# Batch 1's third and fourth pair of heads: k and v loaded through GpSimd's DMA queue instead of SyncE's

## The chip, the core and the metric

The kernel runs on one core of a Trainium2 chip. The core has a matrix engine (PE, or TensorE), a vector engine (DVE), a scalar engine (ACT), GpSimd (POOL) and SyncE (SP), each with its own stream of instructions that it works off in order. They meet through semaphores. DMAs are issued by instructions on SP, ACT or POOL; each issuer has its own queue. The metric is the time on the device in microseconds; a run here is compared by the median of several executions.

## What is computed

The reference is a linear attention with a norm, followed by a feed-forward layer:

```python
batch, n_heads, seq, head_dim = (8, 8, 576, 64)
kv  = np.einsum('bhsd,bhse->bhde', k, v)
out = np.einsum('bhsd,bhde->bhse', q, kv)
rms = np.sqrt(np.mean(out * out, axis=-1, keepdims=True) + 1e-06)
out = out / rms * g_norm
x = out.transpose(0, 2, 1, 3).reshape(4608, 512)
h = x @ w_in                      # 512 -> 2048
g = np.maximum(0.01 * h, h)
return g @ w_out                  # 2048 -> 512
```

The weights come as 64-bit floats and are rounded to 32 bits by the kernel itself.

## The kernel before

**Tiling.** The 4608 tokens are nine blocks of 512 rows. A batch has 576 tokens, so a block's x takes one batch's outputs and a piece of the next. The eight heads of a batch are four pairs: `load_pair(b, p)` loads k, v and q of pair p of batch b. A k or v load is 288 KB into a tile of the tags `k_in` and `v_in` (`in_tile`, two buffers of each); q goes in four pieces into `q_in`. Each of these loads is a DMA on SP's queue (L130 for k and v through `load_two`, L159 for q). Batch 0 is loaded apart, by `load_first`, over three queues.

**Attention of a batch.** `attention(b, ...)` is a generator; whoever builds the program takes one step of it at a time. It turns q (L455, DVE), multiplies k by v for two pairs at a time (`attention_kv`, 72 PE records that the profile names `kv_ps`), copies the sums to `kv` (`copy_kv`, L324, DVE), then makes outputs (PE `o_ps`; ACT squares L368 and scaled copies L374 for 448 columns, L416 and L421 for the 128 columns that fall to the next block), and divides by the norm (DVE L372 to L402, ACT L386 and L394). It also asks for the loads of later pairs: after the first two pairs of batch b it asks for pairs 2 and 3 of the same batch, after the last two for pairs 0 and 1 of the next. For batches from 2 on (`apart`) these go into a list, `to_load`, that is worked off one by one. Batch 1 is the only one with `apart=False`: it asks for its pairs 2 and 3 at once, in the step after the first kv group.

**The first block.** `first_block` works on block 0 in the plain way, in sixteen steps n = 0 to 15, since the weights are still coming in. Step n makes `h_ps` from x and one w1 tile (128 of the 2048 columns), ACT applies the leaky relu (L1055), and one step later four accumulators `o_acc` take the product with one w2 tile. Between the steps, `between(n, half)` runs: it takes a step of attention (batch 0's tail, then batch 1 at the places 12 to 28), issues weight loads on SP (L220) and rounds weights that have landed.

**The weights.** There are 32 tiles (16 of w1, 16 of w2). A raw tile is 512 KB, and there are seven homes for raw tiles, three in `stage`, four in `pairs`. `round_f64` turns a raw tile into the 32-bit tile: ACT reads it twice (L247, L245, into `add` and `cut`), DVE makes four steps of it (L249, L253, L255, L258). A w1 tile is a part of `w1_all`, called `w_all` in the profile; w2 tiles are called `w`. The last tiles in order are those of w1 for n = 14, w2 for 13, w1 for 15, w2 for 14, w2 for 15.

**The sums on POOL.** From block 1 on, the products are made in Strassen's way, with seven products for eight. The weight sides for it are sums of tiles (`add`, L636), which POOL makes in the homes that raw tiles leave: `sides_w1`, `sides_w2`, `combine`. The sums that are needed again go to DRAM from SP's queue (L685, L723 to L727).

**What sets the order.** The order of PE's matmuls, of the loads, and of the four rounding steps is pinned to the program. Where `in_turn` and `add` do not pin (they pin only once `steady` is true, from block 2 on, or for `in_line`), a scheduler places the instructions of DVE, ACT and POOL by its own estimate of when their inputs come. So the order on these engines between the pinned instructions is no part of the text of the kernel.

Of the kernel before, what the change touches and what calls it, by code (L numbers as in the profile page):

```python
# [23 lines left out]
def kernel(  # L24
# [36 lines left out]
    nc = tc.nc  # L61
# [31 lines left out]
    def in_turn(ins):  # L93

        if steady or in_line:
            pin(ins)
# [24 lines left out]
    k_ins, v_ins, q_ins = {}, {}, {}  # L121

    def half_of(p, i):


        return i ^ (p & 1)

    def load_two(eng, src, t):

        pin(eng.dma_start(t.rearrange("p j d -> p (j d)"),  # L130
                          src.rearrange("h (p j) d -> (h p) (j d)", j=J)))
        return t

    def in_tile(name):
        return ins.tile([P, J, D], F32, tag=f"{name}_in", name=f"{name}_in")
# [3 lines left out]
    def load_some(n=1):  # L139

        while to_load and n > 0:
            b, p, what = to_load.popleft()
            load_pair(b, p, what)
            n -= 1

    def load_pair(b, p, what="kvq"):


        if "k" in what:
            k_ins[b, p] = load_two(nc.sync, k[b, 2 * p:2 * p + 2], in_tile("k"))  # L150
            v_ins[b, p] = load_two(nc.sync, v[b, 2 * p:2 * p + 2], in_tile("v"))
        if "q" not in what:
            return
        t = ins.tile([P, T * D], F32, tag="q_in", name="q_in")
        for l in range(2):
            for c in range(2):
                r0, n = 64 * l + 32 * c, T * D - 32 * c
                src = q[b, 2 * p + half_of(p, l)].rearrange("(t s) d -> t (s d)", s=T)
                pin(nc.sync.dma_start(t[r0:r0 + 32, :n], src[:, 32 * c:]))  # L159
        q_ins[b, p] = t  # L160
# [151 lines left out]
    def attention_kv(b, m, kv_ps):  # L312

        two = [(k_ins.pop((b, p)), v_ins.pop((b, p)), p) for p in (2 * m, 2 * m + 1)]
        for j in range(J):
            for i in range(2):
                for k_in, v_in, p in two:
                    r, c = 64 * i, 64 * half_of(p, i)
                    matmul(kv_ps[p % 2][c:c + 64], lhsT=k_in[r:r + 64, j, :],
                           rhs=v_in[r:r + 64, j, :], start=(j == 0), stop=(j == J - 1))  # L320

    def copy_kv(b, kv_ps):
        for i in range(2):
            in_turn(nc.vector.tensor_copy(kvs[b % 2][:, i::2, :], kv_ps[i]))  # L324
# [14 lines left out]
    def kv_tiles():  # L339
        return [ps_att.tile([P, NP // 2, D], F32, tag="att", name="kv_ps") for _ in range(2)]  # L340
# [83 lines left out]
    def tail_of(b, lo, hi, fine=False, kv=(None, None)):  # L424
        sums = []
        if hi - lo <= N2:
            both_outputs(b, lo, hi, sums, kv[0])
            yield
            if kv[1] is not None:
                kv_beside(b + 1, kv[1], att_tiles("kv_ps"))  # L430
            yield
        else:
            for e in range(2):
                outputs(b, lo, hi, e, sums, kv[e])
                yield
        for _ in divide(lo, hi, sums):
            if fine:
                yield
        if not fine:
            yield  # L440
# [3 lines left out]
    def kinds(b):  # L444
        return ("q",) if b > KV_BESIDE else ("q", "kv")

    def attention(b, apart=True, fine=False):

        qT = qTs[b] = work.tile([P, NP, S], F32, tag="qT", name="qT")
        beside = b > KV_BESIDE  # L450
        kv_ps = None if beside else kv_tiles()

        def turn(p):
            q_in = q_ins.pop((b, p))
            in_turn(nc.vector.transpose(  # L455
                qT[:, p, :].rearrange("p (t s) -> p s t", s=T),
                q_in.rearrange("p (s d) -> p s d", d=D)[:, :, :32]))

        for m in range(2):
            turn(2 * m)  # L460
            yield
            turn(2 * m + 1)
            if m:
                yield
            if kv_ps:
                attention_kv(b, m, [t[:, m, :] for t in kv_ps])
            pairs_next = [(b + m, p) for p in ((2, 3) if m == 0 else (0, 1)) if b + m < B]
            if b == KV_BESIDE and m:
                to_load.extend((b + 1, p, "kv") for p in range(2))
            if apart or m == 0:  # L470
                for nxt in pairs_next[:1 if apart else 2]:
                    if apart:
                        to_load.extend((*nxt, what) for what in kinds(b + m))
                    else:
                        load_pair(*nxt)
            yield
            if apart:
                if m and kv_ps:
                    copy_kv(b, kv_ps)
                for nxt in pairs_next[1:]:  # L480
                    to_load.extend((*nxt, what) for what in kinds(b + m))
                yield
        if not apart:
            copy_kv(b, kv_ps)
            yield
        kv = [(None, None), (None, None)]
        if KV_BESIDE <= b < B - 1:
            kv = [(None, None), (0, 1)] if b > KV_BESIDE else [(None, 0), (None, 1)]
        tails = [tail_of(b, max(i * NT, b * S), min((i + 1) * NT, (b + 1) * S), fine, kv[i - b])
                 for i in (b, b + 1)]  # L490
        if not fine:
            for tail in tails:
                yield from tail
            return

        for tail in (0, 0, 0, 0, 0, 1, 0, 0, 1, 1, 1, 1, 1, 1):
            next(tails[tail])
            yield
# [538 lines left out]
    def first_block(between):  # L1037
# [28 lines left out]
        for t in range(4):  # L1066
# [3 lines left out]
            else:  # L1070
# [3 lines left out]
    first_attention()  # L1074
    steps = {i: tail for tail in [tail_of(0, NT, S)] for i in (6, 8, 10)}
    a_steps = attention(1, False)
    steps.update((i, a_steps)
                 for i in (12, 13, 15, 16, 18, 20, 22, 23, 24, 26, 28))
    loaded, rounded = 7, 5

    def between(n, half):
        nonlocal loaded, rounded
        go(steps.get(2 * n + half, iter(())), 1)

        while half and rounded < min(3 * n + 8, 2 * n + 13, len(w_jobs) - (n < 11)):
            if loaded < len(w_jobs):
                load_w(loaded)
                loaded += 1
                if loaded in (15, 19):
                    load_pair(1, (loaded - 15) // 4)  # L1090
            round_w(rounded)
            rounded += 1
        if (n, half) == (12, 0):
            for p in range(2):
                load_pair(2, p)
# [38 lines left out]
    for i in range(1, NB):  # L1134
        one = i == 1
        steady = not one
        late, a_steps = a_steps, attention(i + 1, fine=not one) if i + 1 < B else iter(())
        os = {}
        for c in range(NC):
# [113 lines left out]
```

## Time and profile before

| what | value |
|---|---|
| median of 8 runs | 917.81 us (915.93 to 922.62) |
| the profiled execution's own time | 918.2 us |
| its span | 916.5 us |
| granted TensorE clock | 1.0 of full |
| PE busy, 70 to 90 us | 18.07 of 20 us |
| PE busy, 90 to 142 us | 52.00 of 52 us |
| PE busy, 230 to 900 us | 669.86 of 670 us |
| DMA engines busy, 105 to 142 us | 49% |
| POOL busy, 70 to 90 us | 0.00 us |
| POOL busy, 105 to 142 us | 16.33 of 37 us |

The span runs from the first to the last instruction of the program; the profiled execution's time has 1.7 us more around it. Times within the span are counted from its start. A line of a timeline has the start and the length in us, the engine, the line of the kernel, the operation, what it writes and reads, and the number of instructions merged; what ended the idle time before it stands in brackets. The matmul lengths are modelled and overlap, so distances from start to start are the safer measure on PE.

The stretch of 27 to 142 us is first_block. Up to about 110 us the DMA engines are full: weights, and batches 1 and 2, come in one after another. From 142 us on PE has work without a gap up to the end.

### The profile page before, as it was taken

How to read it: one execution, taken by the hardware profiler on the slowest of the kernel's cores; microseconds unless marked ns; L12 is line 12 of the kernel's file. 1: busy time of each engine (PE TensorE's matmuls, PEld its weight loads, DVE VectorE, ACT ScalarE, POOL GpSimd, SP SyncE). 2: the span in 40 equal slices, each digit the busy share in tenths (PEclk: the TensorE clock that was granted, in tenths of full speed). 3: DMA queues.
4: the chain of work that ended last, by engine and by line, in shares of the span. 5: the costliest groups of instructions: out<-in, count | busy, mean ns of one | idle time of the engine just before them, and what ended most of it. 6: DMA issues, size and time to landing. Idle time of an engine off the chain costs nothing.

```text
span 916.5 us, 18030 instructions
## 1 busy us (share of the span) xinstructions
PE 908.6 (99%) x6976; PEld 775.7 (85%) x6976; DVE 633.0 (69%) x1168; ACT 328.4 (36%) x645; POOL 370.0 (40%) x438
## 2 busy tenths in 40 slices
PE   8999999999999999999999999999999999999998
PEld 5444447888998999899999999999999999999997
DVE  5876995587457876587756786678659755755565
ACT  5454433242135233433243323332443333223330
POOL 2000354977633473226421642264226422642222
PEclk9999999999999999999999999999999999999999
DMA  8999926895599778766886789658755676666632
GB/s 260 234 252 217 271 82 192 275 304 167 169 351 289 230 212 266 235 229 213 257 258 217 221 249 272 221 174 207 249 181 176 190 222 198 183 190 222 198 108 92
DMA packets 90229, 200.06 MB, mean 218 GB/s; under 512 B 9888, under 2 KB 42272, under 8 KB 90144
## 3 DMA queue, kind: packets, MB, share of 16 engines
q1 hardware_dynamic: 79680, 187.04, 69.1%
q10 hardware_dynamic: 10016, 10.69, 3.4%
q8 instruction: 56, 0.92, 0.4%
q0 software_dynamic: 448, 1.18, 0.3%
q14 instruction: 29, 0.24, 0.1%
HBM read 172.39 MB, written 26.48 MB: 217 GB/s over the span
## 4 chain that ended last, share of the span: by engine, by line
PE 89%; DMA 8%; DVE 1%; ACT 1%; issue 0%; POOL 0%; ACTq 0%; DVEq 0%; SPq 0%; POOLq 0%
PE o_a L118 19%; PE o_c L118 18%; PE h_ha L118 11%; PE h_hb L118 11%; PE h_hc L118 8%; PE h_hd L118 8%; PE o_acc L118 3%; PE o_ps L118 3%; DMA stage<-in_moe_w_in_dram 2%; PE h_ps L118 2%; DMA pairs<-in_moe_w_in_dram 2%; PE h_a L118 2%; PE h_b L118 2%; DMA q_in<-in_q_dram 1%; PE h_c L118 1%; PE h_d L118 1%
## 5 line engine op out<-in xcount | busy, mean ns | idle before, releaser
L636 POOL TENSOR_TENSOR gs<-g 128x512 f32<-128x512 f32 x64 | 81.7, 1278 | 253.6 <-ACT g L832 253.6
L832 ACT ACTIVATE g<-g 128x512 f32<-128x512 f32 x124 | 78.2, 631 | 130.6 <-DVE g L636 130.6
L951 ACT COPY w_all<-h_ha 128x512 f32<-128x512 f32 x84 | 48.9, 582 | 173.6 <-PE h_ha L118 167.9
L118 PE MATMUL o_a<-pairs,gs 128*128 128x256 f32 x384 | 91.3, 381 | 0.0
L118 PE MATMUL o_c<-pairs,gs 128*128 128x256 f32 x376 | 89.2, 380 | 0.0
L636 DVE TENSOR_TENSOR o<-h_hb,o 128x128 f32<-128x128 f32 x104 | 29.8, 286 | 83.9 <-ACT pairs L951 83.8
L636 DVE TENSOR_TENSOR o<-o_c,o 128x512 f32<-128x512 f32 (+1 forms) x91 | 61.1, 672 | 23.9 <-PE o_c L118 23.6
L118 PEld LDWEIGHTS o_a<-pairs,gs 128*128 128x128 f32 x384 | 69.8, 190 | 9.2 <-POOL pairs L636 1.2
L118 PEld LDWEIGHTS o_c<-pairs,gs 128*128 128x128 f32 x376 | 68.3, 190 | 7.7
L636 DVE TENSOR_TENSOR o<-o_a,o 128x512 f32<-128x512 f32 x75 | 51.2, 683 | 28.2 <-PE o_a L118 28.1
L636 POOL TENSOR_TENSOR pairs<-w_all 128x512 f32<-128x512 f32 x8 | 11.0, 1378 | 120.4 <-DMA stage<-in_moe_w_in_dram 93.3
L118 PE MATMUL h_ha<-stage,w_all 128*128 128x128 f32 x448 | 59.6, 276 | 0.0
L118 PEld LDWEIGHTS h_ha<-stage,w_all 128*128 128x128 f32 x448 | 56.6, 192 | 3.0 <-issue 0.7
L118 PE MATMUL h_ps<-xT,w_all 128*128 128x512 f32 (+1 forms) x136 | 58.0, 570 | 0.3 <-DVE w_all L258 0.3
L118 PE MATMUL o_acc<-w,g 128*128 128x512 f32 x128 | 57.8, 595 | 0.0
L636 DVE TENSOR_TENSOR g<-g,pairs 128x512 f32<-128x512 f32 x84 | 55.6, 689 | 1.9
L636 POOL TENSOR_TENSOR pairs<-g 128x128 f32<-128x128 f32 x52 | 23.7, 456 | 75.4 <-PE h_hb L118 46.7
L118 PEld LDWEIGHTS h_ps<-xT,w_all 128*128 128x128 f32 x136 | 25.5, 190 | 29.4 <-issue 26.6
L636 DVE TENSOR_TENSOR w_all<-h_hc,w_all 128x512 f32<-128x512 f32 x56 | 38.3, 684 | 15.9 <-PE h_hc L118 15.6
L118 PEld LDWEIGHTS o_acc<-w,g 128*128 128x128 f32 x128 | 24.0, 190 | 29.8 <-issue 29.4
L636 DVE TENSOR_TENSOR o<-h_hd,o 128x128 f32<-128x128 f32 x78 | 22.1, 283 | 37.9 <-ACT pairs L951 37.8
L118 PE MATMUL h_hb<-stage,w_all 128*128 128x128 f32 x336 | 46.7, 275 | 0.0
(228 smaller groups left out, 2265.2 us busy)
## 6 DMA issues: line engine op xcount, KB each, us to landing
w_all<-w SPq DMA_DIRECT2D x196, 448.0 KB, 4.2
pairs<-w SPq DMA_DIRECT2D x56, 512.0 KB, 4.3
out_dram<-o ACTq DMA_DIRECT2D x35, 256.0 KB, 4.7
v_in<-in_v_dram SPq DMA_DIRECT2D x29, 288.0 KB, 5.3
k_in<-in_k_dram SPq DMA_DIRECT2D x28, 288.0 KB, 4.8
q_in<-in_q_dram SPq DMA_DIRECT2D x56, 144.0 KB, 6.3
q_in<-in_q_dram SPq DMA_DIRECT2D x56, 140.0 KB, 6.4
w<-stage SPq DMA_DIRECT2D x12, 512.0 KB, 4.6
```

Of the source, the lines that this page charges most:

```text
L118: pin(nc.tensor.matmul(*args, **kw))
L636: ins = eng.tensor_tensor(out_, a, b_, op=ALU.subtract if minus else ALU.add)
L832: nc.scalar.activation(t, t if src is None else src, func=AF.Prelu, alpha=SLOPE)
L951: nc.scalar.copy(q[:, at], bank)
```

## The change

`load_pair` gets a parameter for the engine that issues the k and v loads. Only one call gives it a value: the one for `apart=False`, so pairs 2 and 3 of batch 1. Their four loads of 288 KB (k and v of each pair) are issued by GpSimd; the q loads of these pairs stay on SP, as do all other loads.

```diff
-    def load_pair(b, p, what="kvq"):
+    def load_pair(b, p, what="kvq", eng=nc.sync):
 
         if "k" in what:
-            k_ins[b, p] = load_two(nc.sync, k[b, 2 * p:2 * p + 2], in_tile("k"))
-            v_ins[b, p] = load_two(nc.sync, v[b, 2 * p:2 * p + 2], in_tile("v"))
+            k_ins[b, p] = load_two(eng, k[b, 2 * p:2 * p + 2], in_tile("k"))
+            v_ins[b, p] = load_two(eng, v[b, 2 * p:2 * p + 2], in_tile("v"))
...
                     if apart:
                         to_load.extend((*nxt, what) for what in kinds(b + m))
                     else:
-                        load_pair(*nxt)
+                        load_pair(*nxt, eng=nc.gpsimd)
```

## The prediction

> **What bounds the kernel now.** I read the page first: span, busy time by engine, and the chain that ended last.
>
> ```profile
> span 916.5 us, 18030 instructions
> PE 908.6 (99%) x6976; PEld 775.7 (85%) x6976; DVE 633.0 (69%) x1168; ACT 328.4 (36%) x645; POOL 370.0 (40%) x438
> PE 89%; DMA 8%; DVE 1%; ACT 1%; issue 0%; POOL 0%; ACTq 0%; DVEq 0%; SPq 0%; POOLq 0%
> ```
>
> PE is busy for 99% and holds 89% of the chain. So the change is worth what it takes from PE's waits, less the waits that it makes. Next the chain of waits of the first 200 us, for the place where the moved loads stand on it.
>
> ```profile
> 80.69 8.69 DMA v_in<-in_v_dram
> 89.38 0.14 issue
> 89.52 1.27 PE kv_ps L118 x70
> 90.79 3.63 PE o_acc L118 x8
> ```
>
> The fourth pair's v is on the chain: issued at 80.69, landed at 89.38. The timeline of PE shows what that costs, and the dates by which the last weights must be rounded.
>
> ```profile
> 68.69 1.28 PE L118 MATMUL kv_ps<-v_in,k_in 64*64 64x64 f32 x72
> 69.90 3.70 PE L118 MATMUL h_ps<-xT,w_all 128*128 128x512 f32 x8
> ...
> 87.27 0.33 PE L118 MATMUL kv_ps<-v_in,k_in 64*64 64x64 f32 x2
> 89.52 1.27 PE L118 MATMUL kv_ps<-v_in,k_in 64*64 64x64 f32 x70 [1.93 <-DMA v_in<-in_v_dram]
> 90.72 3.70 PE L118 MATMUL o_acc<-w,g 128*128 128x512 f32 x8
> ...
> 131.60 3.60 PE L118 MATMUL h_ps<-xT,w_all 128*128 128x512 f32 x8
> 135.04 7.03 PE L118 MATMUL o_acc<-w,g 128*128 128x512 f32 x16
> ```
>
> 72 kv matmuls take 1.21 us from start to next start (68.69 to 69.90); these take 3.45 (87.27 to 90.72). The wait is therefore worth 2.24 us, and between 27 and 900 us it is the only wait of PE over 0.15 us. At 131.60 the sixteenth step of first_block (n = 15) needs its w1 tile; at 135.04 and 138.47 the o_acc groups of n = 14 and 15 need their w2 tiles. I call these W1(15), W2(14) and W2(15). Last, the timelines of DVE and POOL in that stretch.
>
> ```profile
> 120.10 0.69 DVE L258 CUSTOM_DVE_ANT_0 w_all<-w_all,add 128x1024 uint16<-128x1024 uint16 x1
> 122.91 1.76 DVE L255 SCALAR_TENSOR_TENSOR w<-cut,w 128x512 uint32<-128x512 uint32 x1
> 126.00 1.75 DVE L258 CUSTOM_DVE_ANT_0 w<-w,add 128x1024 uint16<-128x1024 uint16 x1
> 131.21 1.21 DVE L258 CUSTOM_DVE_ANT_0 w<-w,add 128x1024 uint16<-128x1024 uint16 x1
> ```
>
> ```profile
> 122.05 2.07 POOL L636 TENSOR_TENSOR pairs<-w_all 128x512 f32<-128x512 f32 x1 [10.16 <-ACT cut L245]
> ```
>
> W1(15) is ready at 120.8, 10.8 us early; W2(14) at 127.75, 7.3 early; W2(15) at 132.4, 6.1 early. Beside POOL's sums (122 to 135.6 us) a rounding step takes 1.75 us instead of 0.69. This slack is what the change can eat.
>
> **What the Trainium skill says.** "SBUF — State Buffer", "Who interferes with whom": DVE in a two-port mode, or with two SBUF inputs, shuts GpSimd out for a whole instruction and the other way round. The trace agrees: L255 0.69 us alone, 1.76 beside POOL's sum, while DVE's transposes keep their 0.64. The same section says that a DMA on GpSimd's queue can be starved, since its descriptors are written by GpSimd. No run here shows it yet: the POOL issues of before stand at 1.35 to 6.4 us, 0.53 to 0.70 us each, beside a nearly idle DVE. "DMA: Bandwidth & Descriptors", "Issuing engines are not separate DMA queues": all queues share the same 16 engines. The trace agrees so far that loads from 15 to 110 us land one behind the other at about 240 GB/s.
>
> **The change part by part.** *The loads.* Four loads of 288 KB leave SP's queue; no byte goes. On POOL's queue they wait for k_in's and v_in's buffers, which the 72 matmuls at 68.69 free at 70.0. POOL is empty from 6.4 to 99.7 us, so nothing is behind them but the sums of L636. Four issues of 0.6 us end at 72.4. SP's queue then holds about 8 us of loads (landing up to 80.7). The four take 1.45 us each alone (landing steps of k_in and v_in), 2.9 shared, with 2 us of latency: 72.4 + 2 + 11.6 = about 86, against PE's need at 87.3. If descriptors are blocked by DVE, which rounds without a break from 67 to 79.5, add up to 1 us an issue: 88 at worst. I take 2.24 us saved (bounds 1.2 and 2.24). SP's remaining loads come at about the same time, since the sum of bytes before them is unchanged, and SP loses four issues of 0.35. Weights loaded at 70 to 80 come up to 6 us later, but ACT reads them at 81 to 92 only, held by L1055, which waits for PE.
>
> *The order.* The two built programs differ in more than the loads. PE's order is the same. On ACT and DVE the scheduler now puts batch 1's attention tail ahead of the last weights. On ACT, the readings (L247, L245) of W1(13) and W2(12) stand behind the first xT pair (L374) instead of ahead of it; those of W1(14) and W2(13) behind the second; those of W1(15), W2(14) and W2(15) behind the last xT copies (L421) instead of at 114.3 to 122. On DVE the tail (L372 to L402, L418) and block 1's differences (L636 xt, xT) come ahead of the roundings. On POOL one sum of a weight side or of g slips ahead of the last stage sum of a combine. Nothing is added; all of it costs by its place. With PE 2.24 us earlier, from rows of the trace:
>
> - ACT ends the first L374 pair at 107.77 - 2.24 = 105.5, reads W1(13) in 1.24 (as 98.38 to 99.62): 106.8.
> - DVE rounds W1(13) in 4.40 (100.67 to 105.07, beside the same three POOL sums, which the same reading releases): 111.2.
> - Then W2(12), two L372, two L382, two L383: 5.18 (113.09 to 118.27), plus 1.92 for two POOL sums beside them (1.39 + 1.65 at 109.37 and 110.80 instead of 0.43 + 0.69): 118.3.
> - W1(14) with L390: 2.5, as 118.27 to 120.80: 120.8. Here before had already W1(15).
> - W2(13) with two L400 and two L402, POOL idle: 0.36 + 0.56 + 0.36 + 1.01 + 0.62 + 0.56 + 0.62 + 1.01 = 5.1 (durations less the 0.07 by which neighbours overlap): 125.9.
> - ACT's last square waits for the second L400 (124.3); it and two copies take 0.8 (129.26 to 130.05), then three tiles are read at 1.15: W1(15) 126.3, W2(14) 127.4, W2(15) 128.6. The last one releases POOL's sums, in before at 122.05.
> - DVE from 125.9: two L418 and three differences 0.4 + 3 x 0.61, W1(15)'s first two steps 0.71: 128.8. Its last two meet POOL's 128x512 sums, 1.7 each as at 122.91 and 126.00: 132.2. PE wants it at 131.60 - 2.24 = 129.4. **First new wait: 2.8** (0.8 with POOL absent).
> - W2(14) ends as seventh of the eight steps left; from 126.00 to 133.07 seven steps took 7.1 beside POOL: 139.3. PE arrives at 132.2 + 3.43 = 135.6. **Second new wait: 3.7** (0 with POOL absent: 3.3 for seven steps). W2(15) follows at 140.3, needed at 142.7.
> - Batch 2's second kv group at 169.30 has v landed at 169.06: 0.24 of slack. The slipped POOL sum (1.3) holds an L727 write, and v queues behind it on SP: **1.0 more** (0 to 1.3).
>
> Sum: -2.24 + 2.8 + 3.7 + 1.0 = +5.3. PE has no later waits that would take it up again. On the profiled execution 918.2 (span 916.5 and 1.7 around it) + 5.3 = 923.5; the median 917.81 is 0.4 lower: **923.1 us**.
>
> **The rivals.** 0.3% (2.75 us) is about what a measurement of this kernel can tell from no change.
>
> *Not slower: the roundings still come in time.* Place: DVE from 125.9 to 139. Price: a step at 0.35 to 0.65 us instead of 1.0 to 1.75. It decides if W1(15) is ready by 129.4 and W2(14) by 132.8, for instance because POOL's sums come after them. For it: the slack of 6 to 11 us. Against: W2(15)'s reading releases POOL just then, and three tiles of rounding stand behind 118.3. Gain alone: 917.81 - 2.24 = 915.6, no change by the bound.
>
> *The loads come too late on the new queue.* For it: starved descriptors, shared engines. Against: about 1 us of margin. The wait at 87.3 then stays or moves by a little; later stages shift with PE, so the new waits stay: up to 917.81 + 7.5 = 925.3.
>
> *One new wait only*, with the lock met half as often: -2.24 + 2.8 + 1.0 = +1.6: 919.4.
>
> **How the numbers follow.** Two new waits 0.66 (923.1); loads late as well 0.12 (925.3); one wait 0.08 (919.4); in time 0.14 (915.6). The range leaves out the last and little else: 918.5, below the one-wait case, to 927.0, above late loads with the extra wait at its bound. Faster 0.03, out of the in-time case with a wait elsewhere gone; same 0.16, from 0.11 in time and 0.05 of one wait; slower 0.81.
>
> **What would show it.** The kv wait at 87 to 89 us gone or under 1 us; k_in and v_in issued by POOL at 70 to 73 and landed by 88. PE waiting for DVE's L258 ahead of h_ps at about 132 and ahead of o_acc at about 139. POOL's sums starting near 128.6. From 230 us on, the same distances between groups as before, all shifted. Wrong if PE has no wait between 125 and 142: then the lock or the scheduler's order is not what I take it for.

## The result, and the profile after

| | before | after |
|---|---|---|
| median | 917.44 us (32 runs) | 927.1 us (11 runs, 925.40 to 929.78) |
| the profiled execution | 918.2 us, span 916.5 | 930.16 us, span 928.4 |
| mean granted clock, profiled execution | 1.0 | 0.994 |
| PE busy, 230 to 900 us | 669.86 of 670 us | 669.86 of 670 us |

The ratio of after to before is 1.0096, 95% interval 1.0079 to 1.0113 (the two medians alone give 1.0105): by the medians slower by 9.7 us, where 5.3 were forecast. The median lies 0.1 us above the upper end of the range; 1.0096 of the 917.81 that the forecast started from is 926.6, just inside it.

The page of after first: its span, the busy line, and the row of the clock in 40 slices.

```profile
span 928.4 us, 18030 instructions
PE 913.9 (98%) x6976; PEld 777.9 (84%) x6976; DVE 633.5 (68%) x1168; ACT 328.2 (35%) x645; POOL 370.5 (40%) x442
PEclk9999998999999999999999999999999999999999
```

PE is busy 5.3 us longer than before with the same 6976 records, and one slice of the clock's row (139 to 162 us) has an 8. So not all of the loss is waiting; a part is matmuls that ran slower. The timeline of PE after:

```profile
87.45 1.28 PE L118 MATMUL kv_ps<-v_in,k_in 64*64 64x64 f32 x72
88.66 3.70 PE L118 MATMUL o_acc<-w,g 128*128 128x512 f32 x8
...
131.47 3.70 PE L118 MATMUL h_ps<-xT,w_all 128*128 128x512 f32 x8 [1.76 <-DVE w_all L258]
139.49 10.18 PE L118 MATMUL o_acc<-w,g 128*128 128x512 f32 x16 [4.32 <-DVE w L258]
149.51 1.89 PE L118 MATMUL h_a<-xT,w_all 128*128 128x256 f32 x8
...
176.91 0.32 PE L118 MATMUL kv_ps<-v_in,k_in 64*64 64x64 f32 x2
179.41 1.89 PE L118 MATMUL kv_ps<-v_in,k_in 64*64 64x64 f32 x70 [2.18 <-DMA v_in<-in_v_dram]
181.24 2.96 PE L118 MATMUL h_d<-xT,pairs 128*128 128x256 f32 x8
```

The 72 kv matmuls at 87.45 now run without a wait (1.21 us to the next start, as against 3.45 before). Then there are three waits: for W1(15), for W2(14), and for batch 2's v. The same groups before, behind the o_acc group at 135.04:

```profile
141.90 1.89 PE L118 MATMUL h_a<-xT,w_all 128*128 128x256 f32 x8
...
169.30 1.28 PE L118 MATMUL kv_ps<-v_in,k_in 64*64 64x64 f32 x72
170.51 1.99 PE L118 MATMUL h_d<-xT,pairs 128*128 128x256 f32 x8
```

So two groups are slow with nothing to wait for: the sixteen o_acc records take 10.02 us from start to next start (139.49 to 149.51), 6.86 before (135.04 to 141.90); the h_d group at 181.24 has 2.96, before 1.99. The windows view shows why. Its columns are the stretch, its length, the busy time of each engine, then the granted clock.

```profile
core 0: us, PE busy (x) PEld busy (x) DVE busy (x) ACT busy (x) POOL busy (x), PEclk, DMA share, GB/s
138.90:145.70 6.80, 6.21 (x8) 2.63 (x9) 2.74 (x3) 0.00 (x0) 2.85 (x3) 0.50 0.00 0
...
179.80:183.20 3.40, 3.40 (x66) 2.92 (x56) 0.49 (x2) 0.63 (x1) 0.62 (x1) 0.50 1.08 352
```

The clock stands at half from 138.86, near the end of the second wait, and from 179.82, just behind the third, and at 1.0 everywhere else between 6 and 927 us. Its records give the two stretches as 6.83 us and 3.41 us.

If the same matmul is followed through both profiles, the distance between after and before moves like this: -2.24 at the old kv wait, +1.93 at 131 us (first wait), +4.58 at 139 us (second wait), +3.16 over the o_acc group (half clock), nothing up to 177 us, +2.47 at batch 2's kv (third wait), +1.62 over that kv group and h_d (half clock), nothing more to the end. Sum +11.5, and 0.2 is scatter of the first 25 us: 11.7.

The last two views are of POOL and DVE, for the chain that the prediction followed.

```profile
70.47 0.58 POOL L130 DMA_DIRECT2D k_in<-in_k_dram  x1 [64.15 <-DMA pairs<-in_moe_w_in_dram]
71.05 0.55 POOL L130 DMA_DIRECT2D v_in<-in_v_dram  x1
71.60 0.75 POOL L130 DMA_DIRECT2D k_in<-in_k_dram  x1
72.34 0.54 POOL L130 DMA_DIRECT2D v_in<-in_v_dram  x1
...
129.13 1.74 POOL L636 TENSOR_TENSOR pairs<-w_all 128x512 f32<-128x512 f32 x1 [12.53 <-ACT cut L245]
```

```profile
120.64 0.69 DVE L258 CUSTOM_DVE_ANT_0 w_all<-w_all,add 128x1024 uint16<-128x1024 uint16 x1
...
125.19 1.08 DVE L402 TENSOR_TENSOR xT<-xT,inv 128x896 f32<-128x896 f32 x1
...
129.78 1.63 DVE L258 CUSTOM_DVE_ANT_0 w_all<-w_all,add 128x1024 uint16<-128x1024 uint16 x1
...
138.13 2.34 DVE L258 CUSTOM_DVE_ANT_0 w<-w,add 128x1024 uint16<-128x1024 uint16 x2
```

W1(14) is ready at 121.3, the attention tail (L402) at 126.3, W1(15) at 131.4, W2(14) in the middle of the last line, at 139.35. L258 takes 0.69 us before POOL's sums start and 1.63 beside the first two of them.

### The profile page after: what moved, and what is told of

It is laid out like the page before. It is cut to its first block, busy times and chain, and to the rows that moved or that the text cites. A ratio compares the mean times of both kernels' runs of the same rounds, so it can differ in the third digit from the quotient of the medians.

```text
span 928.4 us, 18030 instructions
## 1 busy us (share of the span) xinstructions
PE 913.9 (98%) x6976; PEld 777.9 (84%) x6976; DVE 633.5 (68%) x1168; ACT 328.2 (35%) x645; POOL 370.5 (40%) x442
## 4 chain that ended last, share of the span: by engine, by line
PE 91%; DVE 5%; DMA 2%; ACT 1%; issue 0%; POOL 0%; SPq 0%; ACTq 0%; DVEq 0%; POOLq 0%
PE o_a L118 18%; PE o_c L118 18%; PE h_ha L118 11%; PE h_hb L118 10%; PE h_hc L118 8%; PE h_hd L118 8%; PE o_acc L118 5%; PE h_ps L118 4%; PE o_ps L118 3%; PE h_a L118 2%; PE h_c L118 1%; PE kv_ps L118 1%; PE h_b L118 1%; PE h_d L118 1%; DMA pairs<-in_v_dram 1%; DMA v_in<-in_v_dram 1%
## 5 line engine op out<-in xcount | busy, mean ns | idle before, releaser
L636 DVE TENSOR_TENSOR o<-h_hb,o 128x128 f32<-128x128 f32 x104 | 29.8, 286 | 83.3 <-ACT pairs L951 83.2
L118 PE MATMUL o_acc<-w,g 128*128 128x512 f32 x128 | 61.0, 623 | 4.3 <-DVE w L258 4.3
L951 ACT COPY pairs<-h_hb 128x384 f32<-128x384 f32 x84 | 40.0, 476 | 13.7 <-PE h_hb L118 12.9
```

Of the source, the lines that this page charges most:

```text
L118: pin(nc.tensor.matmul(*args, **kw))
L636: ins = eng.tensor_tensor(out_, a, b_, op=ALU.subtract if minus else ALU.add)
L951: nc.scalar.copy(q[:, at], bank)
```

## The experiments

Two devices are used. One puts an engine's instructions into a given order: for each pair of neighbours in a list of instruction numbers, the second is issued behind the first. PE's order is never changed. The other puts work or a wait at one place. The runs were made in three groups of four. Those of a group share a chip and the runs of the kernel before there: medians of before were 918.85 us (the first four runs), 918.65 (the next four) and 919.26 (the last four).

```diff
     while go_o():
         pass
+    ORDERS = (
...
+    )
+    made = {i.name: i for i in nc.cur_bb.bb.instructions}
+    for order in ORDERS:
+        for prev, ins in zip(order, order[1:]):
+            tc.add_manual_dep(made[f"I-{ins}"], f"I-{prev}",
+                              mybir.DependencyInfo(mybir.DependencyClass.NoSync,
+                                                   mybir.DependencyReason.DATA), reason="order")
```

**The queue without the order.** The changed kernel, with three lists (DVE, ACT, POOL) that hold the order of before.

> The four loads stay on GpSimd's queue; every instruction of DVE, ACT and POOL is issued in the order of the kernel before. Order theory (the loads save the 2.24 us wait and all of the loss comes from the order on DVE, ACT and POOL): 915.2 us, 0.9975 of before, no wait of PE for L258 near 130 to 140 us, the granted clock 1.0 throughout. Queue theory (four loads written by GpSimd disturb it or the other transfers, and the order is a side effect): 922 us or more.

Measured: 917.13 us against 918.85, ratio 0.9968, interval 0.9952 to 0.9984. Its PE timeline:

```profile
89.02 1.28 PE L118 MATMUL kv_ps<-v_in,k_in 64*64 64x64 f32 x72
90.23 3.70 PE L118 MATMUL o_acc<-w,g 128*128 128x512 f32 x8
...
134.55 7.03 PE L118 MATMUL o_acc<-w,g 128*128 128x512 f32 x16
...
169.38 1.27 PE L118 MATMUL kv_ps<-v_in,k_in 64*64 64x64 f32 x70 [0.24 <-DMA v_in<-in_v_dram]
```

No wait for v at 89, none for L258 at 131 or 135, and 0.24 us at batch 2. The queue theory falls: the four loads on GpSimd's queue cost nothing that can be seen, and the wait that they were to remove is gone. This version has the lowest ratio of the study. How much that is in time depends on what it is set against: of the 36 executions of before beside it, the 22 at full clock have a median of 917.56 us, only 0.4 more, and the other 14, with a mean clock of 0.998 or 0.996, take 920.69 us or more.

**The order without the queue.** The kernel before, with three lists that hold the order of after.

> The four loads stay on SP's queue as in the kernel before; DVE, ACT and POOL have the order of the changed kernel. Order theory: the old wait of 2.24 us for v is back and the chain from it starts 2.24 us later, so 929.3 us (927.1 + 2.2), with waits for L258 near 133 and 141 us. Queue theory: 917.4 us, as before.

Measured: 934.96 us, ratio 1.0162, interval 1.0128 to 1.0196. The two L258 waits are there (1.75 us at 138.6, 4.32 us at 146.7), in a kernel whose loads were not touched. So the order alone makes them. But the time is 5.7 us above the 929.3 expected. PE at batch 1's second kv group, and the clock there:

```profile
87.53 0.33 PE L118 MATMUL kv_ps<-v_in,k_in 64*64 64x64 f32 x2
92.01 2.19 PE L118 MATMUL kv_ps<-v_in,k_in 64*64 64x64 f32 x70 [4.15 <-DMA v_in<-in_v_dram]
94.14 5.39 PE L118 MATMUL o_acc<-w,g 128*128 128x512 f32 x8
```

```profile
90.80:97.50 6.70, 5.49 (x74) 3.55 (x75) 3.16 (x8) 0.74 (x2) 0.00 (x0) 0.50 0.95 226
```

In the profiled execution the loads of the first 80 us came later: v was issued at 84.01 instead of 80.69, and the old wait was 4.15 us instead of 1.93, with 6.83 us of half clock from 90.74. That is 2.2 + 3.4, and with 929.3 it makes 934.9; that this comes so close is in part luck, since the third wait is shorter here (1.51 us, at full clock). The order can't have delayed this load, for the first instruction of DVE that stands elsewhere in it is `copy_kv` (L324), at 94.24, and those of ACT and POOL come later still. Why the loads came late is not shown. The other five executions were not profiled: four have mean clocks of 0.993 or 0.995, and the one at 0.998 took 928.80 us, near the 929.3.

**Work in the second wait.** The changed kernel with its own order, and matmuls whose sums nobody reads in front of the o_acc group of n = 14: four of them, one, and two.

```diff
             between(n, 0)
+            if n == 15:
+                idle = ps_m.tile([P, NT], F32, tag="ha", name="idle_ps")
+                for _ in range(4):
+                    matmul(idle, lhsT=x[:, 0, :P], rhs=x[:, 0, :], start=True, stop=True)
             for t in range(4):
```

> The changed kernel with four more matmuls of 512 columns (3.43 us, nobody reads their sums) on PE ahead of the o_acc group of n = 14, in the stretch where it waits 4.3 us for W2(14); all orders as in the changed kernel. Clock theory (the idle of 4.3 us is what makes the granted clock fall to half at 138.9 to 145.7 us): the wait is 0.9 us long, the o_acc matmuls come 429 ns apart, and the kernel takes 3.1 us less than the changed one, about 924.0 us. Rival (the clock falls for another reason, or its fall is in this one profile only): 927 us as the changed kernel.

> As the run with four more matmuls in the wait for W2(14), but with one of them: 0.86 us of work, so that PE is idle for 3.4 us. If only an idle of well over 3.4 us makes the clock fall, no stretch of half clock at 138 to 146 us and the time of the run with four. If a stretch of 3.4 us that is mostly idle is enough, half clock there in nearly all executions, as in the changed kernel: mean clock 0.996 to 0.998, about 927 us.

> The same with two of them: 1.72 us of work and an idle of 2.6 us. If the idle must cover a whole stretch of 3.4 us: mean clock 1.0 but for the third wait, about 925 us. If a stretch that is mostly idle is enough, half clock in a part of the executions, with both values of the time, 925 and 927, among them.

Each of the matmuls leaves two records. The second column is read from the profile of each version.

| matmuls added | idle of PE that is left | median | ratio, interval | executions with a mean clock of 0.998 or less |
|---|---|---|---|---|
| 0 (first sample) | 4.32 us | 927.1 us | 1.0096, 1.0079 to 1.0113 | 12 of 12 |
| 0 (again, as a base) | 4.32 us | 928.03 us | 1.0106, 1.0081 to 1.0131 | 6 of 6 |
| 1 | 3.38 us | 926.78 us | 1.0069, 1.0043 to 1.0094 | 6 of 7 |
| 2 | 2.52 us | 926.77 us | 1.0073, 1.0046 to 1.0099 | 5 of 7 |
| 4 | 0.81 us | 925.41 us | 1.0068, 1.0040 to 1.0096 | 1 of 7 |

PE with four of them, and the clock in the stretch that was at half in after:

```profile
135.13 3.60 PE L118 MATMUL idle_ps<-xT 128*128 128x512 f32 x8
139.53 7.13 PE L118 MATMUL o_acc<-w,g 128*128 128x512 f32 x16 [0.81 <-DVE w L258]
```

```profile
138.90:145.60 6.70, 6.07 (x14) 2.77 (x15) 3.57 (x4) 0.33 (x1) 2.98 (x4) 1.00 0.23 78
```

The o_acc group starts at the same time as in after (139.53 against 139.49), for W2(14) is no earlier; but its records come 429 ns apart, and the group takes 6.97 us instead of 10.02. A group that is given more work ahead of it and takes 3 us less is explained by the clock alone. That the whole kernel became faster is less sure: the median is 1.7 us lower than in the first sample, on another chip, about 1.4 us above the 924.0 expected, and the intervals of the ratios overlap. The count of executions at half clock and the profile carry the verdict. With one matmul the clock still fell (its profile has 3.41 us of it, from 140.67). With two, 5 of 7 executions have a stretch of half clock, though the profiled one has none; since the third wait (1.4 to 1.8 us in these profiles) can bring one too, they can't all be put to the 2.52 us. The last section shows on what it depends.

**POOL's sums out of the way.** The changed kernel with its own order, and one more wait: POOL's sums from `sides_w1` on start when W2(15) is rounded.

```diff
+    tc.add_manual_dep(made["I-1158"], "I-1028",
+                      mybir.DependencyInfo(mybir.DependencyClass.Sync,
+                                           mybir.DependencyReason.DATA), reason="hold")
```

> The changed kernel, all orders kept, but POOL's sums from sides_w1 on start only when W2(15) is rounded. Lock theory (the last roundings are late because they meet POOL's sums; without these a step takes 0.35 to 0.7 us): first wait about 0.9 us, second wait 0, no half clock after it; with the third wait and its half clock left, 919 to 921 us. Rival (the place behind the attention tail alone makes them late): both waits as in the changed kernel, 927 us.

Measured: 919.59 us, ratio 1.0008, interval 0.9989 to 1.0026. PE, then DVE:

```profile
130.37 3.70 PE L118 MATMUL h_ps<-xT,w_all 128*128 128x512 f32 x8 [0.82 <-DVE w_all L258]
133.91 7.03 PE L118 MATMUL o_acc<-w,g 128*128 128x512 f32 x16
```

```profile
129.63 0.69 DVE L258 CUSTOM_DVE_ANT_0 w_all<-w_all,add 128x1024 uint16<-128x1024 uint16 x1
130.24 0.76 DVE L249 TENSOR_SCALAR cut<-cut 128x512 f32<-128x512 f32 x2
...
132.78 1.29 DVE L258 CUSTOM_DVE_ANT_0 w<-w,add 128x1024 uint16<-128x1024 uint16 x2
```

POOL starts at 134.20 instead of 129.13. W1(15)'s last step takes 0.69 us instead of 1.63; the eight steps behind it take 3.8 us (130.24 to 134.07) instead of 9.1. The second wait is gone, the first is 0.82, and the third is 0.98 us at full clock. Holding work back gave some 8 us. Of the 6.1 us that PE waited for roundings, only 0.8 stay when these don't meet POOL's sums.

**POOL's order alone.** The changed kernel; DVE and ACT keep its order, POOL gets that of before.

> The changed kernel with POOL's order of the kernel before (ACT and DVE as in the changed one): the sum that slipped ahead of the last stage sum goes back. Slip theory (the third wait is the 1.0 us of the prediction, set by that sum alone): third wait under 1.2 us instead of 2.2, 1.0 to 1.3 us less than the changed kernel, up to 3 if the half clock behind it goes as well. Store theory (SP's writes of the sums come in a bunch at 150 to 160 us, because one of them waits for the semaphore that ACT's store of out also counts on): less than 0.5 us of it, the third wait stays near 2 us.

Measured: 925.97 us, ratio 1.0078, interval 1.0055 to 1.0100, beside 928.03 for the changed kernel on the same chip. The third wait there, first in the changed kernel as run again, then with POOL's order of before:

```profile
176.18 0.33 PE L118 MATMUL kv_ps<-v_in,k_in 64*64 64x64 f32 x2
178.27 2.06 PE L118 MATMUL kv_ps<-v_in,k_in 64*64 64x64 f32 x70 [1.77 <-DMA v_in<-in_v_dram]
```

```profile
176.81 0.33 PE L118 MATMUL kv_ps<-v_in,k_in 64*64 64x64 f32 x2
177.63 1.27 PE L118 MATMUL kv_ps<-v_in,k_in 64*64 64x64 f32 x70 [0.50 <-DMA v_in<-in_v_dram]
```

From 1.77 to 0.50 is 1.27 us, and the half clock behind this wait is gone. The sum that stands ahead of the last stage sum on POOL in after has the same length:

```profile
161.41 1.27 POOL L636 TENSOR_TENSOR pairs<-w_all 128x512 f32<-128x512 f32 x1
162.65 0.73 POOL L636 TENSOR_TENSOR stage<-pairs,stage 128x256 f32<-128x256 f32 x1
```

SP's next write (L727, at 163.40) waits for the second of them, and v is issued behind it. But that the two numbers are equal is chance. In the changed kernel as run again v is issued 3.99 us ahead of the first kv matmul and lands 5.95 us after its issue; with POOL's order of before it is 4.71 and 5.40. So 0.72 us come from the issue, the rest from a shorter landing.

**The stores of out.** In the trace of after, SP's write L726 is issued at 149.93 instead of 126.25: it waits for a semaphore on which ACT's stores of `out` (L1072) count too, and these land at about 150. All later writes of sums come in a bunch behind it. Was that the third wait? The changed kernel with its own order, and the four stores issued by GpSimd between two of its sums, where it is idle:

```diff
-            nc.scalar.dma_start(out[t * P:(t + 1) * P, :], o)
+            nc.gpsimd.dma_start(out[t * P:(t + 1) * P, :], o)
```

> The changed kernel, orders kept, with the four stores of out at the end of first_block (L1072) issued by GpSimd between two of its sums instead of by ACT, so that no write of SP shares a semaphore with them. Store theory: the writes of w1 sums (L725 to L727, L723) leave at 133 to 143 us instead of 150 to 160, batch 2's second v lands 1.5 to 2 us earlier against PE, the third wait is under 0.8 us with no half clock behind it: 1.5 to 3.2 us less than the changed kernel. Slip theory: the third wait stays over 1.3 us, less than 1 us gained.

Measured: 926.74 us, ratio 1.0097, interval 1.0070 to 1.0125. SP's queue and PE:

```profile
135.08 0.46 SPq L726 DMA_DIRECT2D w<-pairs  x1
```

```profile
180.67 1.27 PE L118 MATMUL kv_ps<-v_in,k_in 64*64 64x64 f32 x70 [1.68 <-DMA v_in<-in_v_dram]
```

The write leaves 15 us earlier, and the third wait stays at 1.68. The store theory falls.

**Both hands on POOL.** The hold and POOL's order of before, together; ACT and DVE keep the order of the changed kernel.

> The changed kernel with both hands on POOL: its order is that of the kernel before, and its sums from sides_w1 on start only when W2(15) is rounded; ACT and DVE keep the order of the changed kernel. If the order on ACT and DVE costs only by meeting POOL's sums, 2.24 us are saved, 0.8 to 1.0 lost in the wait for W1(15) and 0 to 0.5 in the third wait: 917 to 918 us on a chip whose kernel before takes 918.7, ratio 0.998 to 0.999. If the order on ACT and DVE costs by itself, over 1.001.

Measured: 918.09 us, ratio 0.9976, interval 0.9963 to 0.9990: the waits are 0.83 us for W1(15) and 0.78 for batch 2's v, the clock 1.0 throughout. ACT and DVE still have the order that the change brought, and the kernel is a little faster than before by the ratio; the 25 executions of before that ran at full clock have a median of 918.20, the same. Against the hold alone the third wait falls only from 0.98 to 0.78: v is issued 5.07 us ahead of the first kv matmul instead of 4.01, but takes 6.04 us to land instead of 5.18. Whether ACT's order or DVE's sets the late roundings wasn't tried: each of the two waits for the other, so that a list of before on one and of after on the other would leave both waiting.

**The program's order.** A fix without lists: everything that ACT and DVE do for attention during first_block is pinned to the order of the text.

```diff
-            nc.scalar.activation(sq, o_ps[l], func=AF.Square)
+            in_turn(nc.scalar.activation(sq, o_ps[l], func=AF.Square))
...
+    in_line = True
     first_block(between)
-    first_done = True
+    in_line, first_done = False, True
```

> The four loads on GpSimd's queue, and everything that ACT and DVE do for attention during first_block pinned to the program's order (in_line true from the start to the end of first_block), so that the scheduler can't put the attention tail ahead of the roundings. Order theory: all waits near 131, 139 and 179 us gone, as with the order of the kernel before: 0.997 of before, within 0.0015 of the run with the forced order. Rival (the program's order is worse than the scheduler's in another place): a wait of PE for x, kv or L418 ahead of 142 us, 0.999 or more.

Measured: 943.2 us, ratio 1.0271, interval 1.0247 to 1.0295. The line of PE that says why:

```profile
126.55 1.94 PE L118 MATMUL o_ps<-qT,kv 64*32 64x448 f32 x16 [23.05 <-DVE kv L324]
```

The text has all roundings up to W2(15) ahead of batch 1's `copy_kv` (L324), so the copy waits until the last weights have come in and been rounded. The interleaving that the scheduler made in the kernel before is worth keeping; the order of the text isn't it.

**The kernel before, again.**

> The kernel before itself, for its spread: some of its executions show a mean clock of 0.998 or 0.996 and take 921 us or more. If that is the same thing as in the changed kernel, the profile of such an execution has a wait for v near 89 us that is longer than 1.93 us, with a stretch of half clock of 3.4 or 6.8 us behind it; an execution at 1.0 has neither.

Measured: 919.16 us, 916.17 to 926.30, ratio to the runs beside it 0.9998, 0.9977 to 1.0019; 8 of 22 executions have a mean clock of 0.998 or 0.996, all of them at 920.68 us or more, and all others at 919.89 or less. The profiled one is at 1.0:

```profile
87.41 0.33 PE L118 MATMUL kv_ps<-v_in,k_in 64*64 64x64 f32 x2
88.30 1.27 PE L118 MATMUL kv_ps<-v_in,k_in 64*64 64x64 f32 x70 [0.56 <-DMA v_in<-in_v_dram]
```

The wait for v was 0.56 us here and 1.93 in the profile that the prediction was made from. A profile of the kernel before with half clock was not obtained; that those eight have a long wait for v, as the run with the order of after has (4.15 us), is likely but not shown. Those at full clock need not have a short one: the wait of 1.93 us in the first profile left the clock at 1.0.

## Why the prediction was right in sign, and short in size

**The loads: as forecast.** 2.24 us were to be saved; between the two profiles 2.24 are. That is against one execution of before; with the wait of 0.56 us in its other profile there was less to save. The issues ended at 72.9 (forecast 72.4), v landed at 83.2 by the trace (forecast about 86). The doubt of the Trainium skill, "SBUF — State Buffer", "Who interferes with whom", that descriptors could be starved, cost nothing here: 0.54 to 0.75 us an issue.

**The chain on ACT and DVE: as forecast.**

| step | forecast | trace |
|---|---|---|
| ACT has read W1(13) | 106.8 | 106.8 |
| DVE: W1(14) ready | 120.8 | 121.3 |
| DVE: attention tail done | 125.9 | 126.3 |
| POOL's sums start | 128.6 | 129.1 |
| W1(15) ready; first wait | 132.2; 2.8 | 131.4; 1.9 |
| W2(14) ready; second wait | 139.3; 3.7 | 139.35; 4.6 |

W1(15) came 0.8 us earlier because only the last of its steps was drawn out (1.63 us; the one ahead of it took 0.68), not the last two. The seven steps from there to W2(14) took 7.9 us, where 7.1 were taken, so its date came out right by luck: two errors of 0.8 us cancelled. With that date right, what the first wait lost in size the second gained: 6.5 us together, forecast and measured. The bounds with POOL absent (0.8 and 0) are what holding POOL back gave: 0.82 and none. So the rival "the roundings still come in time" named the right switch, but in the changed kernel POOL does start just there.

**The third wait: the slip as forecast, the landing left out.** 1.0 us was taken for the slipped sum, 2.47 came in the first profile. SP's queue before shows the issue of v:

```profile
164.19 0.43 SPq L130 DMA_DIRECT2D v_in<-in_v_dram  x1
```

After, the chain of waits shows its issue and its landing together:

```profile
172.68 6.60 DMA v_in<-in_v_dram
```

Before, v is issued 5.11 us ahead of the first kv matmul (169.30); after, 4.23 us ahead (176.91). That is 0.9 us, near the 1.0. But it lands 6.60 us after its issue, and before it was 4.87: another 1.7 us, for which the forecast had no term. Less the slack of 0.24 they make 2.4. In the runs with POOL's order of before v is issued 4.71 to 5.18 us ahead and lands in 5.40 to 6.04 us, which leaves waits of 0.24 to 0.78. What sets the landing time was not found; moving the stores and with them the bunch of writes left it at 5.86 us.

**The step that failed is the sum**: "-2.24 + 2.8 + 3.7 + 1.0 = +5.3. PE has no later waits that would take it up again." It prices a wait of PE at its own length and every matmul at the length it had before. The term that is missing is the clock: in both profiles of the changed kernel it was at half for 6.83 us at the second wait and for 3.41 us at the third, and the matmuls there took about twice as long. In the first profile that is 3.16 + 1.62 = 4.8 us. All 18 executions of the changed kernel have mean clocks from 0.998 to 0.993, which is one stretch of 3.41 us or more; one costs 1.7 us. With -2.24 + 1.93 + 4.58 + 2.47 = +6.7 for the waits, one to three stretches give 8.4 to 11.8, and the median moved by 9.7. So of the 4.4 us by which the forecast was short, about 1.4 are the waits of the first profile (6.7 instead of 5.3), nearly all of it the third one's landing, and the rest fits the clock.

This could have been foreseen. The Trainium skill has it, in "TensorE: Matmul & The Clock Gate", "Part 1: The HAM clock gate": the clock is gated to half after an idle window of about 3.4 us, and comes back after a busy one; the windows run freely. The stretches of 3.41 and 6.83 us and the clock of 0.50 agree. A forecast of a 3.7 us wait should have carried the price of a window or two with it. The page's limit does not agree: its "HAM oscillation" section warns of gaps of more than about 3.4 us, while here half clock followed a wait of 3.38 us, and a third wait of 1.77 or 2.18 us in two profiles. The measurement decides: a window of which 2.2 of the 3.4 us are idle is enough (worked out in the last section).

**The later course: as forecast.** From 230 to 900 us PE is busy for 669.86 us in both, and the shift of 11.7 us stays to the end.

## What to carry to other kernels

Where a scheduler places instructions, an edit at one place can move others 40 us later: compare the order of the two programs on each engine before pricing the edit, and hold on to the order that was good (here the same edit gives 0.9968 with it and 1.0096 without). Here a wait of TensorE of 2.2 us or more cost, besides itself, half of the 3.4 us stretch behind it, once or twice, unless it lay astride two steps of the clock; if such a wait can't go, matmuls that nobody reads can keep the clock up. When late work shares its time with another engine's sums, try holding those sums back before moving the late work.

## What the runs showed of the hardware that was not expected

- The clock changes on a grid. The records of after have it at 1.0 for 133.12 us from 5.74 on, at 0.5 for 6.83, at 1.0 for 34.13, at 0.5 for 3.41, and at 1.0 for 744.11: 39, 2, 10, 1 and 218 steps of 3.413 us. In the 13 profiles with such records, PE's waits up to its last matmul, laid over their own grids, fall into two kinds. Each of the nine steps at full clock in which PE waited 2.18 us or more was followed by half clock; none with 1.76 us or less was, and of two with 1.77 us one was. Half clock ended with the first step in which PE did not wait.
- So the place of a wait matters as well as its length. With two matmuls added, a grid point at 138.51 cut the wait (137.09 to 139.61) into 1.42 and 1.10 us, and the clock stayed at 1.0. With one added, 2.97 us of the wait (136.84 to 140.22) lay in one step, and the clock fell at its end, 140.67. The wait of 1.93 us in the profile of before was cut into 0.91 and 1.02 us.
- In the four programs whose profile has a wait of 4.32 us, all 36 executions have a mean clock of 0.998 or less; with 3.38 us left it was 6 of 7, with 2.52 us (and a third wait of 1.7) 5 of 7, with 0.81 us (and a third wait of 1.4) 1 of 7. The first wait of about 1.76 us at 131 us was never followed by half clock in the eight profiles that have it.
- The kernel before spreads from 916.44 to 926.92 us (36 runs beside the first group), 14 of them at 0.998 or 0.996. The same program with the four loads on GpSimd's queue and the order kept spreads from 916.36 to 918.47 (22 runs), none below 0.999. Taking these loads off the queue that the others wait in went with a steadier time, which a single profile of before doesn't show.
